# Attention rewritten inside an mLSTM and hash-routing kernel: masked exponents from one bf16 product, decay carried by q, cross term summed in PSUM, steps issued one ahead

## Chip, cores and metric

The kernel runs on one core of one Trainium2 chip. The metric is device time in microseconds (us), from launch to end. Three runs of the kernel before gave 596.22, 596.9 and 597.88 us, median 596.9.

## What is computed

Two blocks follow one another. The first is an mLSTM cell for 4 batches, 8 heads, 768 time steps and a head size of 40:

```python
m_new = maximum(f[t] + m, i[t])
f_stab, i_stab = exp(f[t] + m - m_new), exp(i[t] - m_new)
C = f_stab * C + i_stab * outer(v[t], k[t])
n = f_stab * n + i_stab * k[t]
y[t] = sigmoid(o[t]) * (C @ q[t]) / maximum(abs(n @ q[t]), 1)
```

The result, 3072 rows of 320 numbers, goes through the second block: `token_id * 2654435761 % 8` picks one of 8 experts for each row, and the row becomes `relu(x @ w1[e]) @ w2[e]` with w1 of 320x1024 and w2 of 1024x320. Everything is float32.

## The kernel before

**Attention (lines 104 to 486).** The recurrence is cut into chunks of 128 time steps, 6 chunks for each batch, so 24 steps (`for s in range(NT)`, line 476; b is the batch, c the chunk). A step treats all 8 heads of a chunk. Within a chunk the recurrence is a masked product: with A the running sum of the log decay and e the log input weight less A, the weight of source t' for target t is exp(A[t] + e[t']) where t >= t'. Between chunks a state C of 40x41 per head is carried (the 41st column is n, since v has a column of ones).

`gates()` (line 163) computes A, e and three exponentials with a head and batch on each of 32 partitions, 768 elements long, and turns them over with TensorE. A is kept as three bf16 pieces whose sum is the float32 value (`thirds`).

A step is issued as follows; one engine runs its own instructions in this order.

- `scores(s)`: eight products k q of 128x128 into PSUM (`sp`, line 264), the four even heads first and the four odd heads after them, 40 rows of the array each; VectorE multiplies them by the weights `w` (`p`, line 266).
- `transposes(s + 1)`: k and q of the next chunk, two heads at a time, eight transposes (`tr`, line 217), copied out by ScalarE (`kqT`, line 220).
- `decays(s + 1)`: eight bf16 products of 128 columns spread A over the partitions (`ab`, line 230); VectorE adds e (line 234), GpSimd cuts the triangle (line 238), ScalarE takes the exponential of 1024 elements (line 242). GpSimd weights k (`kw`, line 245). The output gate's sigmoid is built from a clip, an exponential, an addition and a reciprocal (`eo`, lines 251 to 254).
- `state(s)`: the cross term q C (`cx`, line 277) and the state's increment kw v (`cx`, line 284); VectorE scales the cross term (`hx`, line 287), GpSimd decays C (line 294), VectorE adds (line 303).
- routing work of the second block, hung on certain steps (`pieces`, line 466): constants at step 1, counts at 3, overflow at 4, slots at 5, four tables at 6 to 9 (`tk`, line 451), indices at 10, and the loads of three experts' weights at 12, 14 and 16.
- `attend(s)`: eight products p v (`hp`, line 311), 41 columns each; VectorE adds the cross term, makes the denominator (`den`) and multiplies twice; SyncE stores the 128 rows (`x_rows`).

A product of two float32 matrices takes two instructions; a transpose takes one. Loads are issued by SyncE (`load(s + 3)`, line 478), k, q, v and o in four transfers of 1024 rows of 160 bytes. The order is written out by hand (`manual_schedule`). SyncE waits for one thing at a time, so a load stands behind the store issued before it.

**Experts (lines 488 to 657).** Rows are gathered by index, turned over, sent through layer 1 (lines 529 and 536) and layer 2 (line 565), and scattered. At line 529 two products use 64 rows of the array each, upper and lower half by turns; at line 606 four products use 32 columns each by turns. w2 tiles come from a pool of 6 buffers.

Of the kernel before, what the change touches and what calls it, by code (L numbers as in the profile page):

```python
# [8 lines left out]
F32 = mybir.dt.float32  # L9
# [8 lines left out]
P = 128  # L18
# [4 lines left out]
def kernel(  # L23
# [36 lines left out]
    assert NB * P == S and FB * P == F and D <= DP and H % 2 == 0 and BH <= 32  # L60
# [17 lines left out]
    w2pool = ctx.enter_context(tc.tile_pool(name="w2pool", bufs=EG + 2))  # L78
# [8 lines left out]
    def weights(src1, src2):  # L87
# [13 lines left out]
    def load_weights(e):  # L101
        W[e] = weights(moe_w1[e], moe_w2[e])

    with tc.tile_pool(name="gates", bufs=1) as gp, \
# [4 lines left out]
        NKQ = 4  # L109
        kqs = [gp.tile([P, 2, H, DP], F32, name=f"kq{i}") for i in range(NKQ)]  # L110
        vs = [gp.tile([P, H, D1], F32, name=f"v{i}") for i in range(NKQ)]
        Cs = [gp.tile([P, PR, 2, D1], F32, name=f"C{i}") for i in range(2)]
        f_sb = gp.tile([BH, S], F32, name="f_sb")
        i_sb = gp.tile([BH, S], F32, name="i_sb")
        tok = gp.tile([P, NT], I64, name="tok")
        st = {}

        def load(s):
            b, c = s // NB, s % NB
            d = st[s] = {"kq": kqs[s % NKQ], "v": vs[s % NKQ]}  # L120
            d["o"] = ld.tile([P, H, D], F32, name="o_sb")
            for dst, src in (
                (d["kq"][:, 0, :, :D], k), (d["kq"][:, 1, :, :D], q), (d["v"][:, :, :D], v), (d["o"][:], o_gate),
            ):
# [3 lines left out]
        nc.scalar.dma_start(i_sb[:], i_gate.rearrange("b h s -> (b h) s"))  # L128
        nc.scalar.dma_start(tok[:], moe_token_ids.rearrange("(p t) -> p t", t=NT))
        make_identity(nc, ident[:])  # L130
        for t in kqs:
            nc.gpsimd.memset(t[:, :, :, D:], 0.0)
        for t in vs:
            nc.gpsimd.memset(t[:, :, D:], 1.0)
        for t in Cs:
            nc.gpsimd.memset(t[:], 0.0)
        for s in range(3):
            load(s)

        A_sb = gp.tile([BH, S], F32, name="A_sb")  # L140
        A3 = gp.tile([3 * 32, S], BF16, name="A3")
        sel3 = gp.tile([3 * 32, BH], BF16, name="sel3")
        e_T = gp.tile([P, NB, BH], F32, name="e_T")
        xA_T = gp.tile([P, NB, BH], F32, name="xA_T")
        kw_T = gp.tile([P, NB, BH], F32, name="kw_T")
        dec = gp.tile([P, BH // 2, NB], F32, name="dec")
# [4 lines left out]
        def thirds():  # L151

            nc.gpsimd.memset(sel3[:], 0.0)
            nc.gpsimd.memset(A3[:], 0.0)
            r1 = gp.tile([BH, S], F32, name="r1")
            r2 = gp.tile([BH, S], F32, name="r2")
            nc.vector.tensor_tensor(r1[:], A_sb[:], hi(A_sb), op=ALU.subtract)
            nc.vector.tensor_tensor(r2[:], r1[:], hi(r1), op=ALU.subtract)
            for i, piece in enumerate((hi(A_sb), hi(r1), r2[:])):
                nc.vector.tensor_copy(A3[32 * i : 32 * i + BH, :], piece)  # L160
                nc.vector.tensor_copy(sel3[32 * i : 32 * i + BH, :], ident[:BH, :BH])

        def gates():
            m_sb = gp.tile([BH, S], F32, name="m_sb")
            a_sb = gp.tile([BH, S], F32, name="a_sb")
            keep = gp.tile([BH, S], F32, name="keep")
            nc.vector.memset(keep[:], 1.0)
            nc.vector.memset(keep.rearrange("p (c t) -> p c t", t=P)[:, :, 0:1], 0.0)
            nc.vector.tensor_tensor_scan(m_sb[:], f_sb[:], i_sb[:], NEG, op0=ALU.add, op1=ALU.max)
            nc.vector.memset(a_sb[:, 0:1], 0.0)  # L170
            nc.vector.tensor_add(a_sb[:, 1:], f_sb[:, 1:], m_sb[:, : S - 1])
            nc.vector.tensor_sub(a_sb[:, 1:], a_sb[:, 1:], m_sb[:, 1:])
            nc.vector.tensor_tensor_scan(A_sb[:], keep[:], a_sb[:], 0.0, op0=ALU.mult, op1=ALU.add)
            thirds()
            e_sb, xA_sb, kw_sb = i_sb, f_sb, a_sb
            nc.vector.tensor_sub(e_sb[:], i_sb[:], m_sb[:])
            nc.vector.tensor_sub(e_sb[:], e_sb[:], A_sb[:])
            Ac = A_sb.rearrange("p (c t) -> p c t", t=P)
            nc.vector.tensor_tensor(
                kw_sb.rearrange("p (c t) -> p c t", t=P), e_sb.rearrange("p (c t) -> p c t", t=P),  # L180
                Ac[:, :, P - 1 : P].to_broadcast([BH, NB, P]), op=ALU.add,
            )
            nc.scalar.activation(kw_sb[:], kw_sb[:], AF.Exp)
            nc.scalar.activation(xA_sb[:], A_sb[:], AF.Exp)
            for src, dst in ((e_sb, e_T), (kw_sb, kw_T), (xA_sb, xA_T)):
                tp = ps.tile([P, NB, BH], F32, name="tpg", tag="tr", bufs=2)
                for c in range(NB):
                    nc.tensor.transpose(tp[:, c, :], src[:, c * P : (c + 1) * P], ident[:BH, :BH])
                nc.vector.tensor_copy(dst[:], tp[:])
# [286 lines left out]
        for s in range(NT):  # L476
            if s + 3 < NT:
                load(s + 3)
# [209 lines left out]
```

## Time and profile before

| what | value |
|---|---|
| median of three runs | 596.9 us |
| time of the profiled execution | 594.8 us |
| its span, first to last instruction | 593.1 us |
| PE busy | 515.4 us, 87% |
| DVE busy | 253.3 us, 43% |
| POOL busy | 131.0 us, 22% |
| ACT busy | 96.3 us, 16% |
| mean granted TensorE clock | 0.763 |

PE is TensorE's matmul side, PEld its weight loads, DVE VectorE, ACT ScalarE, POOL GpSimd, SP SyncE. Busy time counts a matmul from its start to its modelled end, so a busy PE may stand at half its clock. The granted clock is a share of 2.4 GHz; 0.50 is the level of 1.2 GHz.

### The profile page before, as it was taken

The page shows a single profiled execution, that of the slowest core. Times are in us where ns is not written, and L with a number is a line of the kernel's source. Part 1 is how long each engine was busy: PE and PEld are TensorE (multiplying, and loading weights), DVE is VectorE, ACT ScalarE, POOL GpSimd, SP SyncE. Part 2 cuts the span into 40 slices and gives each one's busy share as a digit, 9 for nine tenths or more (in the row PEclk, how much of TensorE's full clock was granted, in tenths as well). Part 3 has the DMA queues.
Part 4 walks back from the last instruction along what each step waited for, and adds up shares of the span by engine and source line. Part 5 has one row for each costly group of instructions (what it writes and reads, how often), then busy time and mean ns, then how long its engine had stood idle before and what let it go on. Part 6 is the DMA issues. An engine that isn't in the chain of part 4 may idle for free.

```text
span 593.1 us, 6980 instructions
## 1 busy us (share of the span) xinstructions
PE 515.4 (87%) x2678; PEld 402.6 (68%) x2678; DVE 253.3 (43%) x515; ACT 96.3 (16%) x167; POOL 131.0 (22%) x196
## 2 busy tenths in 40 slices
PE   0799598187669999999999489999999999999994
PEld 0699597177559999898999346565655666656553
DVE  7578568644463786878768321111111111111000
ACT  0331112010111122222221011101111011110110
POOL 2134211220221113221231240304131303010111
PEclk9995656555555656765565579999999999999998
DMA  9123223231122277894500124352513434000000
GB/s 175 17 53 61 55 56 56 55 56 29 28 56 55 56 194 156 228 262 82 102 22 11 55 78 135 110 167 88 188 56 104 145 108 137 11 21 12 22 12 23
DMA packets 120914, 49.52 MB, mean 83 GB/s; under 512 B 101804, under 2 KB 117168, under 8 KB 120880
## 3 DMA queue, kind: packets, MB, share of 16 engines
q1 hardware_dynamic: 118144, 40.64, 28.8%
q0 software_dynamic: 2496, 8.20, 4.4%
q8 instruction: 22, 0.36, 0.2%
q10 hardware_dynamic: 240, 0.22, 0.1%
q14 instruction: 12, 0.10, 0.0%
HBM read 41.18 MB, written 8.19 MB: 83 GB/s over the span
## 4 chain that ended last, share of the span: by engine, by line
PE 71%; DVE 14%; issue 5%; POOL 4%; ACT 3%; DMA 1%; POOLq 0%; ACTq 0%; DVEq 0%
PE mh L536 16%; PE zp L565 15%; PE hp L311 10%; PE sp L264 9%; PE tr L217 6%; PE mh L529 4%; DVE eo L254 4%; PE cx L277 3%; POOL w L238 2%; PE ab L230 2%; PE tk L451 2%; ACT w L242 2%; PE cx L284 1%; DVE w L234 1%; DVE p L266 1%
## 5 line engine op out<-in xcount | busy, mean ns | idle before, releaser
L565 PE MATMUL zp<-w2t,h 128*128 128x320 f32 x384 | 105.2, 433 | 0.0
L536 PE MATMUL mh<-xT,w1t 128*128 128x416 f32 x256 | 98.4, 528 | 0.9 <-issue 0.9
L565 PEld LDWEIGHTS zp<-w2t,h 128*128 128x128 f32 x384 | 72.7, 190 | 32.1 <-issue 3.3
L238 POOL TENSOR_SCALAR_AFFINE_SELECT w<-w 128x512 f32<-128x512 f32 x48 | 31.3, 675 | 227.9 <-DVE w L234 227.9
L311 PE MATMUL hp<-v,p 128*128 128x41 f32 x384 | 76.9, 380 | 2.0 <-DVE p L266 2.0
L536 PEld LDWEIGHTS mh<-xT,w1t 128*128 128x128 f32 x256 | 47.6, 193 | 44.0 <-issue 42.9
L311 PEld LDWEIGHTS hp<-v,p 128*128 128x128 f32 x384 | 73.8, 294 | 3.6 <-DVE p L266 2.5
L518 DVE COPY xT<-tp 128x384 f32<-128x384 f32 x16 | 8.9, 558 | 142.1 <-PE tp L514 102.7
L264 PE MATMUL sp<-kqT 40*128 40x128 f32 x384 | 69.1, 413 | 0.0
L264 PEld LDWEIGHTS sp<-kqT 40*128 40x128 f32 x384 | 62.2, 301 | 1.8 <-ACT kqT L220 0.2
L220 ACT COPY kqT<-tr 128x512 f32<-128x512 f32 x48 | 28.0, 585 | 167.8 <-PE tr L217 167.8
L254 DVE RECIPROCAL eo<-eo 128x320 f32<-128x320 f32 x24 | 51.7, 2153 | 0.8
L217 PE MATMUL tr<-ident,kq 128*128 128x128 f32 x192 | 46.3, 421 | 0.0
L499 POOL DMA_INDIRECT out_dram<-zo,s_idx x26 | 25.6, 985 | 92.6 <-ACT zo L498 92.6
L543 DVE TENSOR_SCALAR h<-mh 128x416 f32<-128x416 f32 x32 | 18.9, 592 | 53.4 <-PE mh L529 26.5
L217 PEld LDWEIGHTS tr<-ident,kq 128*128 128x128 f32 x192 | 36.9, 220 | 5.2 <-issue 5.1
L451 PE MATMUL tk<-oh_c,oh_r 128*128 128x47 f32 x48 | 11.2, 429 | 32.2 <-POOL oh_c L442 32.2
L242 ACT ACTIVATE w<-w 128x1024 f32<-128x1024 f32 x24 | 25.4, 1057 | 71.9 <-POOL w L238 71.9
L234 DVE TENSOR_TENSOR w<-ab,e_T 128x512 f32<-128x512 f32 x48 | 30.8, 684 | 13.9 <-PE ab L230 13.9
L277 PE MATMUL cx<-C,kqT 128*128 128x82 f32 x160 | 35.1, 392 | 0.1
L545 ACT ACTIVATE h<-mh 128x416 f32<-128x416 f32 x32 | 16.5, 517 | 109.6 <-PE mh L529 59.7
L277 PEld LDWEIGHTS cx<-C,kqT 128*128 128x128 f32 x160 | 33.1, 305 | 0.4 <-issue 0.4
(154 smaller groups left out, 442.8 us busy)
## 6 DMA issues: line engine op xcount, KB each, us to landing
w2t<-in_moe_w_dram SPq DMA_DIRECT2D x8, 1280.0 KB, 8.7
w1t<-in_moe_w_dram SPq DMA_DIRECT2D x8, 1024.0 KB, 5.3
kq<-in_k_dram SPq DMA_DIRECT2D x24, 160.0 KB, 2.8
kq<-in_q_dram SPq DMA_DIRECT2D x24, 160.0 KB, 3.4
v<-in_v_dram SPq DMA_DIRECT2D x24, 160.0 KB, 3.6
o_sb<-in_o_gate_dram SPq DMA_DIRECT2D x24, 160.0 KB, 3.6
x_rows<-x SPq DMA_DIRECT2D x24, 160.0 KB, 1.9
w1c<-in_moe_w_dram SPq DMA_DIRECT2D x16, 128.0 KB, 5.4
```

What stands on the lines that cost most here:

```text
L217: nc.tensor.transpose(tp[:, j, :], d["kq"][:, i, 2 * j : 2 * j + 2, :].rearrange("p h d -> p (h d)"), ident[:],)
L220: nc.scalar.copy(d["kqT"][:, i], tp[:])
L234: nc.vector.tensor_tensor(w[:, hf], ab[:], e_T[:, c, b * H + hf : (b + 1) * H : 2].unsqueeze(2).to_broadcast([P, PR, P]), op=ALU.add,)
L238: nc.gpsimd.affine_select(w[:, hf], w[:, hf], compare_op=ALU.is_ge, fill=NEG, base=0, pattern=[[0, PR], [1, P]], channel_multiplier=-1,)
L242: nc.scalar.activation(w[:], w[:], AF.Exp)
L254: nc.vector.reciprocal(d["eo"][:], d["eo"][:])
L264: nc.tensor.matmul(sp[:, j, :], lhsT=kqT[r, 0, j, :], rhs=kqT[r, 1, j, :], start=True, stop=True)
L277: nc.tensor.matmul(cx[:, 2 * j * D1 : (2 * j + 2) * D1], lhsT=d["kqT"][:, 1, j, :], rhs=st["C"][:, j].rearrange("p h d -> p (h d)"), start ...
L311: nc.tensor.matmul(hp[:, h, :], lhsT=d["p"][h % 2][:, h // 2, :], rhs=d["v"][:, h, :], start=True, stop=True)
L499: ins = nc.gpsimd.indirect_dma_start(out=out[:, :], out_offset=bass.IndirectOffsetOnAxis(ap=idx, axis=0), in_=zo[:], in_offset=None, bound ...
L536: nc.tensor.matmul(hp[i][:, :cols], lhsT=w1t[:, db, fb * P : (fb + 1) * P], rhs=xT[:, db, :cols], start=(first and db == 0), stop=(not fir ...
L565: nc.tensor.matmul(zp[:], lhsT=h[:, fb, j * P : (j + 1) * P], rhs=w[2][:, fb, :], start=(fb == 0), stop=(fb == FB - 1),)
```

## The change

- **Exponents and mask in one product.** `Ls` holds on its 128 partitions the pieces of e, rows of ones and a unit matrix; `Rs` holds a head selector, the pieces of A and a table of zeros and -1e30. Four bf16 products of 512 columns give A + e + mask for all heads (`ab`), each filling 64 of the 128 output partitions, and ScalarE takes the exponential straight from PSUM, twice 512 elements. The addition on VectorE and the cut on GpSimd go away. The pieces are written to DRAM (`z_d`) once by `gates()`; `load_e` reads e for each batch, `load_a` A for each step, two transfers.
- **Decay applied to q.** Two more products (`xb`) spread exp(A); VectorE multiplies the turned q by them (`qs`). ScalarE copies the last column as the decay of C (`dec`).
- **Cross term in PSUM.** In `attend(s)` each pair of heads gets the product qs C first and the two products w v are added in PSUM (`xh`, two buffers). `hx` goes away.
- **Scores by turns.** The eight products alternate between upper and lower 64 rows, and read 64 rows (24 of zeros) instead of 40.
- **Output gate.** ScalarE's Sigmoid on up to six chunks at once (five calls); GpSimd divides by the denominator (`gated`), VectorE makes the last product (`finish`).
- **q loaded by batch** in rows of 960 bytes. `pad_q` (VectorE, 320 elements) and `turn_q` take one sixth at a time: all six of batch 0 ahead of the loop, those of the next batch at chunks 0 to 4 of the batch before it (two at chunk 1).
- **Order.** In iteration s, `decays` and `scores` of s + 1 and the transposes of k of s + 2 stand ahead of `attend(s)`; `finish(s - 1)` and its store follow one iteration late. The routing pieces stand behind `attend(s)`.
- **Gates.** The maximum scan stays as it was; the rest runs on 96 partitions of 256 elements, after three transfers that spread m. `tables()` fills `Ls` and `Rs`.
- **w2 tiles** come from two pools of 3, the second opened after attention.

```diff
         def decays(s):
+            R = Rs[s % 2]
             for hf in range(2):
                 ab = ps.tile([P, PR, P], F32, name="ab", bufs=2)
-                for j in range(PR):
+                for i in range(2):
                     nc.tensor.matmul(
-                        ab[:, j, :], lhsT=sel3[:, bh : bh + 1].to_broadcast([3 * 32, P]),
-                        rhs=A3[:, c * P : (c + 1) * P], start=True, stop=True,
+                        ab[i * HB : (i + 1) * HB], lhsT=Ls[b % 2][:, c * P + i * HB : c * P + (i + 1) * HB],
+                        rhs=R[:, i, hf::2, :], start=True, stop=True,
                     )
-                nc.vector.tensor_tensor(
-                    w[:, hf], ab[:], e_T[:, c, b * H + hf : (b + 1) * H : 2].unsqueeze(2).to_broadcast([P, PR, P]),
-                    op=ALU.add,
-                )
-                nc.gpsimd.affine_select(
-                    w[:, hf], w[:, hf], compare_op=ALU.is_ge, fill=NEG,
-                    base=0, pattern=[[0, PR], [1, P]], channel_multiplier=-1,
-                )
-            nc.scalar.activation(w[:], w[:], AF.Exp)
+                nc.scalar.activation(w[:, hf], ab[:], AF.Exp)
+            if c > 0:
+                xb = ps.tile([P, PR, P], F32, name="xb", tag="tr", bufs=2)
+                for hf in range(2):
+                    nc.tensor.matmul(
+                        xb[hf * DP : (hf + 1) * DP], lhsT=Lx[:], rhs=R[:, 0, hf::2, :], start=True, stop=True,
+                    )
+                d["qs"] = wk.tile([P, PR, P], F32, name="qs")
+                nc.vector.tensor_tensor(d["qs"][:], q_of(s), xb[:], op=ALU.mult)
+                d["dec"] = wk.tile([P, PR, 1], F32, name="dec")
+                nc.scalar.copy(d["dec"][:], xb[:, :, P - 1 :])
-            nc.vector.tensor_scalar_max(d["eo"][:], d["o"][:], -88.0)
-            nc.scalar.activation(d["eo"][:], d["eo"][:], AF.Exp, scale=-1.0)
-            nc.vector.tensor_scalar_add(d["eo"][:], d["eo"][:], 1.0)
-            nc.vector.reciprocal(d["eo"][:], d["eo"][:])
...
         def scores(s):
+            for j in range(PR):
+                for hf in range(2):
+                    r = slice(hf * DP, (hf + 1) * DP)
+                    nc.tensor.matmul(
+                        sp[hf][:, j, :], lhsT=d["kT"][r, j, :], rhs=q_of(s)[r, j, :], start=True, stop=True,
+                    )
+            for hf in range(2):
+                nc.vector.tensor_tensor(d["w"][:, hf], sp[hf][:], d["w"][:, hf], op=ALU.mult)
...
         def attend(s):
+            for j in range(PR):
+                if c > 0:
+                    nc.tensor.matmul(
+                        d["xh"][:, 2 * j * D1 : (2 * j + 2) * D1], lhsT=d["qs"][:, j, :],
+                        rhs=st["C"][:, j].rearrange("p h d -> p (h d)"), start=True, stop=False, skip_group_check=True,
+                    )
+                for hf in range(2):
+                    nc.tensor.matmul(
+                        hs[:, 2 * j + hf, :], lhsT=d["w"][:, hf, j, :], rhs=d["v"][:, 2 * j + hf, :],
+                        start=(c == 0), stop=True, skip_group_check=True,
+                    )
+            nc.vector.tensor_scalar(den[:], hs[:, :, D:], scalar1=-1.0, scalar2=1.0, op0=ALU.mult, op1=ALU.max)
+            nc.vector.tensor_tensor(den[:], den[:], hs[:, :, D:], op=ALU.max)
+            nc.vector.reciprocal(den[:], den[:])
...
         for s in range(NT):
             if s + 3 < NT:
                 load(s + 3)
-            scores(s)
-            if s + 1 < NT:
-                transposes(s + 1)
-                decays(s + 1)
-            state(s)
-            for piece in pieces.get(s, []):
-                piece()
-            attend(s)
+            if s + 2 < NT:
+                load_a(s + 2)
...
+            decayed(s)
+            if s > 0:
+                gated(s - 1)
+            if s + 2 < NT:
+                turn_k(s + 2)
+            if b + 1 < B:
+                for r in turns_of.get(c, ()):
+                    pad_q(b + 1, r)
+                    turn_q(b + 1, r)
+            if s + 1 < NT:
+                decays(s + 1)
+            if s > 0 and (s, "all") in og:
+                sigmoid(s)
+            state(s)
+            if s + 1 < NT:
+                k_weights(s + 1)
+            if s > 0:
+                finish(s - 1)
+            if s + 1 < NT:
+                scores(s + 1)
+            attend(s)
+            for piece in pieces.get(s, []):
+                piece()
```

## Rows read from the trace of the kernel before

**Rows 1.** The page: the TensorE clock granted, in 40 slices of 14.8 us, tenths.

```profile
PEclk9995656555555656765565579999999999999998
```

**Rows 2.** The page: shares of the chain that ended last, by engine.

```profile
PE 71%; DVE 14%; issue 5%; POOL 4%; ACT 3%; DMA 1%; POOLq 0%; ACTq 0%; DVEq 0%
```

**Rows 3.** Stages: window and length, busy PE, PEld, DVE, ACT, POOL (instructions), PEclk, DMA, GB/s.

```profile
0.00:21.74 21.74, 3.03 (x20) 2.64 (x21) 14.49 (x25) 2.86 (x3) 3.63 (x18) 1.00 0.75 131
21.74:330.80 309.06, 268.30 (x1685) 254.36 (x1684) 205.60 (x410) 61.96 (x96) 71.10 (x110) 0.58 0.37 81
344.90:593.00 248.10, 240.36 (x962) 143.64 (x962) 29.00 (x67) 30.55 (x66) 49.07 (x60) 0.98 0.26 83
```

**Rows 4.** The chain through one step: start, us on the chain, work.

```profile
217.88 1.90 PE tr L217 x8
219.78 0.85 PE ab L230 x8
220.63 1.74 PE cx L277 x8
222.37 1.01 PE cx L284 x16
223.39 3.57 PE hp L311 x16
226.96 3.02 PE sp L264 x16
```

**Rows 5.** Order of time on PE, 229 to 240 us: start, us busy, work.

```profile
229.91 1.97 PE L217 MATMUL tr<-ident,kq 128*128 128x128 f32 x8
...
234.44 1.98 PE L311 MATMUL hp<-v,p 128*128 128x41 f32 x16
236.35 1.71 PE L264 MATMUL sp<-kqT 40*128 40x128 f32 x16
237.99 1.09 PE L217 MATMUL tr<-ident,kq 128*128 128x128 f32 x8
238.92 0.61 PE L230 MATMUL ab<-A,sel 96*128 96x128 bf16 x8
239.61 1.09 PE L277 MATMUL cx<-C,kqT 128*128 128x82 f32 x8
```

**Rows 6.** Two stretches around a rise of the clock, columns as in group 3.

```profile
229.80:233.20 3.40, 3.40 (x21) 3.23 (x20) 2.55 (x5) 1.17 (x2) 0.04 (x1) 0.50 0.52 109
233.20:236.60 3.40, 3.40 (x40) 3.22 (x40) 1.39 (x4) 1.42 (x2) 2.98 (x4) 1.00 0.75 134
```

**Rows 7.** The chain in the expert stage: products by turns on parts of the array.

```profile
453.72 4.44 PE zp L606 x64
458.16 8.81 PE zp L565 x32
478.13 1.60 PE mh L529 x8
```

**Rows 8.** Groups by line and shape: count | busy us, mean ns | idle before.

```profile
L254 DVE RECIPROCAL eo<-eo 128x320 f32<-128x320 f32 x24 | 51.7, 2153 | 0.8
L251 DVE TENSOR_SCALAR eo<-o_sb 128x320 f32<-128x320 f32 x24 | 10.3, 428 | 0.0
L321 DVE RECIPROCAL den<-den 128x8 f32<-128x8 f32 x24 | 4.9, 203 | 0.8
L242 ACT ACTIVATE w<-w 128x1024 f32<-128x1024 f32 x24 | 25.4, 1057 | 71.9 <-POOL w L238 71.9
L183 ACT ACT_TABLE_LOAD x1 | 1.3, 1283 | 2.5 <-issue 2.5
```

**Rows 9.** Order of time in step 6: a routing table's work on POOL and PE.

```profile
114.76 1.31 POOL L442 TENSOR_TENSOR oh_c<-oh_c,tokv 128x282 f32<-128x282 f32 x1 [4.05 <-DVE oh_c L438]
116.12 2.79 PE L451 MATMUL tk<-oh_c,oh_r 128*128 128x47 f32 x12 [14.51 <-POOL oh_c L442]
```

**Rows 10.** DMA issues: count, KB each, us from issue to landing.

```profile
w2t<-in_moe_w_dram SPq DMA_DIRECT2D x8, 1280.0 KB, 8.7
```

More of the change, by code (lines that the diff above doesn't have):

```diff
@@ L108 @@
          tc.manual_schedule():
-        NKQ = 4
-        kqs = [gp.tile([P, 2, H, DP], F32, name=f"kq{i}") for i in range(NKQ)]
-        vs = [gp.tile([P, H, D1], F32, name=f"v{i}") for i in range(NKQ)]
+        NC2 = NB // 2
+        BC = NC2 * BH
+        HB = P // 2
+        assert NC2 == 3 and BH == 32 and 3 * H <= 32 and DP == HB
+        NK = 4
+        ks = [gp.tile([P, H, DP], F32, name=f"k{i}") for i in range(NK)]
+        vs = [gp.tile([P, H, D1], F32, name=f"v{i}") for i in range(NK)]
@@ L133 @@
+        for t in ks[:3] + qps + kws + ks[3:]:
+            nc.gpsimd.memset(t[:, :, D:], 0.0)
         for t in vs:
@@ L136 @@
             nc.gpsimd.memset(t[:], 0.0)
+        for s in range(2):
+            load(s)
         for s in range(3):
[L138 to L146, printed above, removed]
+            load_o(s)
@@ L174, in gates, with pieces @@
[L174 to L178, printed above, removed]
+            tables()
+            def pieces(t, i0):
+                nc.vector.tensor_tensor(r1[:], t[:], hi(t), op=ALU.subtract)
+                nc.vector.tensor_tensor(r2[:], r1[:], hi(r1), op=ALU.subtract)
+                for i, piece in enumerate((hi(t), hi(r1), r2[:])):
+                    nc.scalar.copy(zt[:, i0 + i, :], piece)
+                nc.scalar.dma_start(z_d[:, i0 : i0 + 3, :], zt[:, i0 : i0 + 3, :])
@@ new lines, with pad_q, turn_q @@
+        nq = [0]
+        def pad_q(b, r):
+            t = qb[b][r] = qps[nq[0] % 2]
+            nq[0] += 1
+            nc.vector.tensor_copy(t[:, :, :D], qb[b]["l"][:, :, r * D : (r + 1) * D])
+        def turn_q(b, r):
+            if r == 0:
+                qb[b]["T"] = wk.tile([P, PR, S], F32, name="qT")
+            t = qb[b].pop(r)
+            tp = ps.tile([P, PR, P], F32, name="tr", tag="tr", bufs=2)
+            for j in range(PR):
+                nc.tensor.transpose(tp[:, j, :], t[:, 2 * j : 2 * j + 2, :].rearrange("p h d -> p (h d)"), ident[:])
+            nc.scalar.copy(qb[b]["T"][:, :, r::NB], tp[:])
@@ L471 @@
         }
+        turns_of = {0: (0,), 1: (1, 2), 2: (3,), 3: (4,), 4: (5,)}
         gates()
-        transposes(0)
+        load_a(0)
+        load_e(0)
+        load(2)
+        for r in range(NB):
+            pad_q(0, r)
+            turn_q(0, r)
+        nc.scalar.dma_start(tok[:], moe_token_ids.rearrange("(p t) -> p t", t=NT))
+        turn_k(0)
+        turn_k(1)
+        load_a(1)
+        load_q(1)
         decays(0)
+        k_weights(0)
+        sigmoid(0)
+        scores(0)
         for s in range(NT):
+            b, c = s // NB, s % NB
             if s + 3 < NT:
                 load(s + 3)
-            scores(s)
+            if s + 2 < NT:
+                load_a(s + 2)
+            for i in range(2):
+                o = s - (s - 3) % 6 + 6 + 2 * ((s - 3) % 6 - 1) + i if s > 2 else 3 + 2 * s + i
+                if o < NT and (s < 3 or 1 <= (s - 3) % 6 <= 3):
+                    load_o(o)
+            if c == 3 and b + 1 < B:
+                load_e(b + 1)
+            if c == 5 and b + 2 < B:
+                load_q(b + 2)
+            decayed(s)
[7 more added lines that the diff above has]
+                    turn_q(b + 1, r)
             if s + 1 < NT:
-                transposes(s + 1)
                 decays(s + 1)
+            if s > 0 and (s, "all") in og:
+                sigmoid(s)
             state(s)
+            if s + 1 < NT:
[5 more added lines that the diff above has]
+            attend(s)
             for piece in pieces.get(s, []):
                 piece()
-            attend(s)
+        gated(NT - 1)
+        finish(NT - 1)
+    w2pools.append(ctx.enter_context(tc.tile_pool(name="w2late", bufs=3)))
     xp = ctx.enter_context(tc.tile_pool(name="xp", bufs=2))
```

288 lines of the change are left out of this document (162 added, 126 removed).

## The prediction

> **What bounds the kernel now.** The chain that ended last is read first: 71% of the span is PE, 14% DVE [rows 2]. The stages come next [rows 3]. The experts' stage, from 344.90 to the end, has PE busy for 240.4 of 248.1 us at a granted clock of 0.98; the change doesn't touch it. The attention loop, 21.74 to 330.80, takes 309.1 us, with PE busy for 268.3 of them, but at a mean clock of 0.58. The slices of the page show it: 5 to 7 tenths through the loop, 9 after it [rows 1]. So the loop is bound by PE running mostly at the 1.2 GHz level, and the rest of its time is PE waiting.
>
> One step is then laid out. At the low level it is a closed row of PE work: 1.90 + 0.85 + 1.74 + 1.01 + 3.57 + 3.02 = 12.09 us [rows 4], the same kinds in every step. At the high level, start to start, hp takes 236.35 - 234.44 = 1.91, sp 1.64, tr 0.93, ab 0.69, and cx 1.09 by its busy time [rows 5]. So a step costs about half there, and what the change does to the clock is worth as much as what it does to the work.
>
> **The sum for the loop, part by part.** All of it is made against the profiled execution, 594.8 us, of which the span is 593.1; the median shown, 596.9, lies 2.1 us above, and these are added at the end.
>
> *Transposes.* Four of k and four of q, as before: 0.95 + 0.95 us low, 0.47 + 0.47 high. Six turns of q go ahead of the loop, so 18 are left in it.
>
> *Exponents (ab).* Before, eight bf16 products of 128 columns, 0.85 us low [rows 4], 0.83 ns a column. Now four of 512 columns, each on half of the array's columns. If two halves run beside one another, 2 x 512 x 0.83 = 0.85 us; one after another, 1.70. The trace shows such work side by side: the four products by turns on 32 columns each cost 4.44/64 = 69 ns apiece, the same 320 columns on the whole array 8.81/32 = 275 [rows 7], and the 16 products of cx at line 284, on 64 columns by turns, 63 ns apiece against hp's 223 [rows 4]. I take 0.85 low, 0.43 high. The two new products xb follow at 0.43 and 0.22.
>
> *Scores.* Four even heads and then four odd ones took 3.02. By turns on the upper and lower 64 rows the nearest row is line 529, 416 columns by halves in 1.60/8 = 200 ns, less than the 275 of 320 columns on the whole array [rows 7]. So 3.02/2 = 1.51 low, 0.82 high; the upper end is no gain at all, 3.02 and 1.64.
>
> *Cross term, increment, hp.* The same products in another order: 1.74, 1.01 and 3.57 low; 1.09, 0.50 (half of 1.01) and 1.91 high.
>
> A full step is thus 11.0 us low and 5.9 high. For the loop, with xb and cross term in 20 steps and the increment in 20: high 24 x (0.47 + 0.43 + 0.82 + 1.91) + 18 x 0.47 + 20 x (0.22 + 1.09 + 0.50) = 87 + 8 + 36 = **131**; low 165 + 17 + 64 = **246**.
>
> *What the other engines must hide.* DVE is busy for 205.6/24 = 8.6 us a step [rows 3]; the reciprocal (2.15) and the clip (0.43) alone [rows 8] bring it to 6.0, and the additions at line 234 go too, so about 5 is left and fits beside 5.9, barely. The cut on POOL leaves the path between product and exponential; POOL keeps three short products. ACT has two copies and two exponentials of 512 elements (under 0.6 each by the 1.057 of 1024) and a share of the sigmoids, 3.5 in all. These edits I cost at nothing while a step lasts 5.9.
>
> The sigmoid makes ACT load its tables anew: five calls, there and back, 10 x 1.28 = 13 us by the row [rows 8], which lie beside PE, as no PE work of the same step waits for a sigmoid. The Trainium skill, in "ScalarE: Activation LUTs", section "What ACT_TABLE_LOAD costs", speaks against this part: exp and sigmoid are in different sets, and a switch costs 2.66 us with its drain. By the page that is 27 us instead of 13; were none of it hidden, the sum would be 542 by the page and 528 by the row. The row shows the 1.28 and no drain.
>
> *A new wait on PE.* `turn_q` waits for `pad_q` on DVE, and that stands behind `den(s - 1)`, which waits for the end of `attend(s - 1)`. Three small operations (0.20 each), the copy of 320 elements (0.43) [rows 8] and some 0.4 of product tail and handoffs, 1.4 us, of which `turn_k` covers 0.47: 1.0 us at 15 steps = **15**. Queued behind `pad_q` are qs, the state's addition and the score product, none needed by PE before the next step.
>
> *Routing pieces, now behind attend.* Tables: PE waits for den (0.6), the compare (0.43), POOL's 1.31 and handoffs, 2.5, then tk takes 2.79 [rows 9]: 5.3 x 4 = 21. At step 6 the wait was 14.51 before. Counts (four operations, a product, a copy) 2.7, slots (ten operations of 192 elements at 0.43 or less) 4.3; constants, overflow and indices fall where PE has no turn of q behind them. Together **28**.
>
> *Start.* Iteration 0 needs w(0). The maximum is spread by transfers, two on SyncE behind some 2.1 MB of loads, which at the stage's 131 GB/s [rows 3] is up to 16 us; I take m at 14. ACT fills the tables (about 8 us by 1.057 per 1024), then makes nine copies of pieces, the exponentials and eight copies of turns; the pieces go to DRAM and come back. I take the loop's start at **33**, between 26 (tables covered by the wait) and 40; now it is 24.5, 21.74 and the first transposes and products.
>
> *Loads.* One step of lead is gone. v(s + 3) waits for attend(s - 1), and k(s + 4), A and o stand behind the store of `finish(s - 1)`. At 12, 14 and 16 they stand behind expert weights (8.7 us to land [rows 10]), against 1.5 steps of lead, about 9 us. I take **5**, between 0 and 30.
>
> *The clock.* Ahead of the rise at 233.20 [rows 6] PE ran transposes [rows 5], then ab and cx without a gap. The new step has these, xb, and scores on both halves of the rows at once, in one stretch, so I expect rises in the first steps and after each stop. In the steps with the longest waits (3 to 10) I expect it to fall again. I take seven steps' worth at the low level, 7 x (11.0 - 5.9) = **36**, between 0 and 115 (all).
>
> Sum: the loop ends at 33 + 131 + 15 + 28 + 5 + 36 = **248** instead of 330.8. What follows (den, gated, last product, store, gathers) is as long as before within 0.5. That is 83 us less: 594.8 - 83 = 512, and with 2.1 and rounding **515**.
>
> **The rivals.** *The clock stays low.* For it: 0.58 now, with PE hardly pausing; the new wait comes once a step. Then 33 + 246 + 15 x 0.5 + 28 + 5 = 320, 586 us (570 to 602). Against it: the rises at 233.20 and elsewhere came from the work that is kept. The Trainium skill, "TensorE: Matmul & The Clock Gate", Part 4 on PE-mode transpose, has a rule that leads here: the full rate does not engage for transposes, as they are not counted as busy in the same way. By that rule the turns bring no rise; the trace disagrees, since the rise came behind eight of them. Chance 0.11.
>
> *Halves one after another* (slower). In ab, xb and sp: at the low level 24 x (0.85 + 1.51) + 20 x 0.43 = 65 more than all-low, 385 and **651** us; at the high level 34 more, 549. It makes the kernel slower once PE is low in about 6 steps of 10; now it is in 8 of 10. Rows 7 and the 63 ns speak against it [rows 4, 7]. Chance 0.05.
>
> *Loads come late.* If each weight load costs 10 us and k, A and o are late elsewhere, 30 instead of 5: 540. For it: SyncE's queue is blocked once a step by the store. Against: DMA share is 0.37 in the loop [rows 3]. Chance 0.10.
>
> *It doesn't do what it says*: routing pieces and `pad_q` still hang on DVE's queue, so PE waits on in the 15 steps. That is in the sum, and in the first rival's size.
>
> **How the numbers follow.** My forecast has 0.74, mostly 490 to 550. The range, 488 to 562, adds late loads and serial halves at the high clock, and half of the loop at the low one (61 instead of 36 us: 540); it leaves out the low-clock case and the slower one. A measurement of this kernel tells apart about 0.3%. Low clock gives half of its 0.11 to faster at least (0.07), 0.02 to same, 0.02 to slower; so faster 0.91, same 0.02, slower 0.07.
>
> **What would show it.** In the changed profile: the loop's end near 248, PEclk mostly 1.00 in it after the first steps; ab as four products with two starting together; sp near half of its time; attend unchanged; PE idle about 1 us before `turn_q`, released by `pad_q`; idle of 2 to 3 us before tk; ACT with 11 table loads and no PE wait on them. Wrong, if PEclk stays near 0.5, if sp still takes 3.0 at the low level, if PE waits for DMA in most steps, or if the first `attend` comes later than 42.

## The result and the profile after

Four runs of the changed kernel gave 497.6 to 505.6 us, median **500.5 us**, beside 596.6 us for the kernel before (four runs): ratio 0.837 (0.833 to 0.842), 96 us less. The forecast, 515 us with a range of 488 to 562, held.

The page of the kernel after, the granted clock in 40 slices of 12.4 us and the chain's shares by engine:

```profile
PEclk9999976677787898799589999999999999999997
...
PE 69%; issue 10%; DMA 8%; DVE 6%; POOL 3%; ACT 2%; SPq 1%; POOLq 0%; ACTq 0%; DVEq 0%
```

Where 5 to 7 tenths stood all through the loop [rows 1], 6 to 9 stand now, and DVE's share of the chain is 6% instead of 14% [rows 2]. DMA and issue have grown.

The stages of the kernel after, columns as in group 3 of the rows above:

```profile
0.00:31.43 31.43, 8.54 (x34) 6.15 (x34) 15.44 (x36) 20.41 (x29) 6.43 (x24) 1.00 0.65 153
31.43:231.00 199.57, 164.54 (x1561) 141.34 (x1561) 99.67 (x261) 77.91 (x124) 48.05 (x82) 0.84 0.52 121
...
249.30:497.00 247.70, 240.21 (x962) 143.63 (x962) 28.98 (x67) 30.56 (x66) 49.05 (x60) 0.98 0.26 83
```

The last row answers to the last of [rows 3]: the experts' stage is as before, 247.7 against 248.1 us, but starts at 249.3 instead of 344.9. So all that changed lies ahead of it. The preparation takes longer: the first score product starts at 32.0 instead of 24.5 us. From there to the last product of `attend` it is 203.2 us instead of 306.3. The same window view over exactly this stretch, called the loop from here on, splits it; before first, then after:

```profile
24.50:330.80 306.30, 265.54 (x1669) 251.86 (x1668) 205.02 (x409) 60.79 (x94) 71.10 (x110) 0.58 0.37 82
32.00:235.20 203.20, 168.17 (x1594) 145.27 (x1592) 100.89 (x265) 77.45 (x124) 48.77 (x83) 0.84 0.51 120
```

PE is busy for 168.2 us instead of 265.5 and idle for 35.0 instead of 40.8. **PE waits hardly less; it does its work in 97 us less**, at a granted clock of 0.84 instead of 0.58.

One step of the kernel after at the high level, PE's instructions in order of time (start, us, work):

```profile
216.11 0.63 PE L285 MATMUL tr<-ident,k 128*128 128x128 f32 x4
216.67 0.62 PE L316 MATMUL ab<-R,L 128*64 128x512 bf16 x4
217.13 0.38 PE L324 MATMUL xb<-R,Lx 128*64 128x512 bf16 x2
217.34 0.61 PE L382 MATMUL xh<-v,kw 128*64 128x41 f32 x16
217.89 1.16 PE L353 MATMUL sp<-qT,kT 64*128 64x128 f32 x16
218.98 0.45 PE L396 MATMUL xh<-C,qs 128*128 128x82 f32 x2
219.26 0.58 PE L401 MATMUL xh<-v,w 128*128 128x41 f32 x4
...
221.68 0.63 PE L285 MATMUL tr<-ident,k 128*128 128x128 f32 x4
```

From start to start: turns of k 0.56, exponents 0.46, `xb` 0.21, increment 0.55, scores 1.09, `attend` 2.70, a step without a turn of q of 221.68 - 216.11 = 5.57 us. The four products of `ab` take 0.46 us at the high level, near the 0.43 that the forecast has for two halves side by side, so the halves run beside one another.

PE's waits from 31 to 240 us of the kernel after (who waits for whom: us in total, times, longest):

```profile
PE tr L301 <- DVE qp L293: 13.8, 8, 6.2
PE tk L544 <- POOL oh_c L535: 9.6, 4, 2.4
PE tr L285 <- DMA k<-in_k_dram: 7.5, 3, 3.1
PE cps L477 <- DVE pr L472: 2.4, 1, 2.4
PE tr L301 <- ACT kT L286: 1.5, 2, 0.8
```

These sum to 34.8 us, nearly all of the loop's idle time. Before, the tables' wait was up to 14.5 us a time [rows 9] and 32.2 us in all by the same view; now it is 2.4 a time, and new waits for `pad_q` and for k have come.

### The profile page after: what moved, and what is told of

It is laid out like the page before. It is cut to its first block, busy times and chain, and to the rows that moved or that the text cites. A ratio compares the mean times of both kernels' runs of the same rounds, so it can differ in the third digit from the quotient of the medians.

```text
span 497.6 us, 6769 instructions
## 1 busy us (share of the span) xinstructions
PE 421.3 (85%) x2604; PEld 297.2 (60%) x2604; DVE 148.7 (30%) x379; ACT 129.8 (26%) x221; POOL 112.1 (23%) x176
## 4 chain that ended last, share of the span: by engine, by line
PE 69%; issue 10%; DMA 8%; DVE 6%; POOL 3%; ACT 2%; SPq 1%; POOLq 0%; ACTq 0%; DVEq 0%
PE mh L673 19%; PE zp L702 18%; PE mh L666 5%; PE xh L401 5%; PE sp L353 4%; PE xh L396 3%; PE ab L316 3%; PE tr L301 3%; DMA R<-gate_pieces 2%; PE xh L382 2%; PE tk L544 2%; PE tr L285 2%; DMA k<-in_k_dram 2%; DMA ql<-in_q_dram 1%; PE tp L649 1%
## 5 line engine op out<-in xcount | busy, mean ns | idle before, releaser
L401 PE MATMUL xh<-v,w 128*128 128x41 f32 x384 | 54.1, 275 | 0.0
L401 PEld LDWEIGHTS xh<-v,w 128*128 128x128 f32 x384 | 49.8, 193 | 0.7 <-issue 0.4
L301 PE MATMUL tr<-ident,qp 128*128 128x128 f32 x96 | 20.9, 368 | 17.0 <-DVE qp L293 15.0
L396 PE MATMUL xh<-C,qs 128*128 128x82 f32 x160 | 34.7, 299 | 0.0
L357 DVE TENSOR_TENSOR w<-sp,w 128x512 f32<-128x512 f32 x48 | 30.8, 683 | 11.1 <-PE sp L353 9.7
L353 PE MATMUL sp<-qT,kT 64*128 64x128 f32 x384 | 32.3, 315 | 0.0
L302 ACT COPY qT<-tr 128x512 f32<-128x512 f32 x24 | 25.2, 1092 | 17.6 <-PE tr L301 17.6
L413 POOL TENSOR_TENSOR og<-og,den 128x320 f32<-128x320 f32 x24 | 17.4, 724 | 54.6 <-DVE den L410 43.8
L353 PEld LDWEIGHTS sp<-qT,kT 64*128 64x128 f32 x384 | 27.5, 217 | 2.9 <-issue 0.4
L328 DVE TENSOR_TENSOR qs<-qT,xb 128x512 f32<-128x512 f32 x20 | 13.8, 688 | 44.5 <-PE xb L324 44.5
L666 PE MATMUL mh<-xT,w1c 64*128 64x416 f32 x128 | 26.7, 535 | 0.0
```

The costliest lines, as they stand in the source:

```text
L301: nc.tensor.transpose(tp[:, j, :], t[:, 2 * j : 2 * j + 2, :].rearrange("p h d -> p (h d)"), ident[:])
L302: nc.scalar.copy(qb[b]["T"][:, :, r::NB], tp[:])
L353: nc.tensor.matmul(sp[hf][:, j, :], lhsT=d["kT"][r, j, :], rhs=q_of(s)[r, j, :], start=True, stop=True,)
L357: nc.vector.tensor_tensor(d["w"][:, hf], sp[hf][:], d["w"][:, hf], op=ALU.mult)
L396: nc.tensor.matmul(d["xh"][:, 2 * j * D1 : (2 * j + 2) * D1], lhsT=d["qs"][:, j, :], rhs=st["C"][:, j].rearrange("p h d -> p (h d)"), star ...
L401: nc.tensor.matmul(hs[:, 2 * j + hf, :], lhsT=d["w"][:, hf, j, :], rhs=d["v"][:, 2 * j + hf, :], start=(c == 0), stop=True, skip_group_che ...
```

## The experiments

The theory of the forecast: the gain is PE's time, shorter scores and above all a higher clock, and VectorE's work costs nothing beside it. The rivals: the gain is the order and VectorE's relief, with PE's own change a small part of it; or the clock answers to something else, such as the rows that the scores read. Ratios are to the kernel before, run on the same chip. The table has, for every kernel, what the window view gives from the first score product to the last of `attend`, in one profiled run of it.

| kernel | time, us | ratio (95%) | loop, us | PE busy | PE idle | clock | DVE busy |
|---|---|---|---|---|---|---|---|
| before | 596.6 | 1 | 306.3 | 265.5 | 40.8 | 0.58 | 205.0 |
| e3_before_64_rows | 591.1 | 0.992 (0.989 to 0.994) | 303.2 | 246.2 | 57.0 | 0.64 | 204.5 |
| e4_before_turns | 585.3 | 0.984 (0.978 to 0.991) | 296.6 | 222.7 | 74.0 | 0.66 | 204.0 |
| e12_before_turns_sigmoid | 523.0 | 0.875 (0.868 to 0.882) | 233.3 | 205.7 | 27.7 | 0.68 | 141.1 |
| after | 500.5 | 0.837 (0.833 to 0.842) | 203.2 | 168.2 | 35.0 | 0.84 | 100.9 |
| e1_heads_in_order | 520.8 | 0.867 (0.857 to 0.877) | 235.9 | 204.3 | 31.6 | 0.75 | 101.6 |
| e2_scores_40_rows | 511.0 | 0.862 (0.854 to 0.869) | 208.1 | 171.7 | 36.4 | 0.83 | 100.5 |
| e5_gate_on_vector | 605.6 | 1.014 (1.007 to 1.020) | 309.2 | 235.6 | 73.6 | 0.64 | 162.8 |
| e8_finish_at_once | 542.6 | 0.912 (0.905 to 0.919) | 241.4 | 179.8 | 61.6 | 0.77 | 100.5 |
| e9_scores_in_own_step | 562.5 | none | 266.4 | 216.0 | 50.4 | 0.67 | 100.9 |
| e11_increment_apart | 529.5 | 0.885 (0.879 to 0.891) | 236.1 | 196.0 | 40.1 | 0.74 | 100.6 |
| e6_pad_early | 488.2 | 0.819 (0.814 to 0.824) | 193.0 | 163.3 | 29.7 | 0.87 | 99.2 |
| e7_tables_early | 485.7 | 0.816 (0.811 to 0.821) | 189.5 | 158.1 | 31.4 | 0.89 | 101.8 |
| e10_all_three | 471.9 | 0.791 (0.786 to 0.795) | 175.3 | 156.6 | 18.7 | 0.90 | 99.0 |

The four runs of e9 lie too far apart (550.8 to 572.3 us) for an interval, and its row of the loop is that of a run of 561 us. Those of e1 span 18 us, and its row is that of a run of 531 us, the longest. The row of e2 is that of its shortest run, 505 us.

**Scores by turns, undone in the changed kernel.**

```diff
-            for j in range(PR):
-                for hf in range(2):
+            for hf in range(2):
+                for j in range(PR):
                     r = slice(hf * DP, (hf + 1) * DP)
                     nc.tensor.matmul(
                         sp[hf][:, j, :], lhsT=d["kT"][r, j, :], rhs=q_of(s)[r, j, :], start=True, stop=True,
```

> The changed kernel with the scores back to four even heads and then four odd ones (still 64 rows each). Theory A (the clock): most of the gain is TensorE's clock, which rises since the step's products now stand in one stretch; the scores by turns are worth their own PE time only. Then sp goes from about 1.1 back to 1.65-1.9 us at the high level, 24 x 0.8 = 20 us more, the clock in the loop stays near 0.84: 515 to 530 us. Rival C (the turns): the two halves side by side are what keeps the array full and the clock high; without them the clock in the loop drops towards 0.6 and the time to 550 us or more.

20 us slower. The groups by line of both kernels (line, tile, count | us busy, mean ns) show the direct part; first after, then e1:

```profile
L353 PE MATMUL sp<-qT,kT 64*128 64x128 f32 x384 | 32.3, 315 | 0.0
```

```profile
L353 PE MATMUL sp<-qT,kT 64*128 64x128 f32 x384 | 49.4, 323 | 0.0
```

One product lasts as long, but side by side they fill 32.3 us instead of 49.4. That is 17 of the 36 us by which PE is busier in this run; the rest goes with the clock, 0.75 instead of 0.84. Over the whole span this run lists 0.866, the other three 0.882 to 0.908 and the runs of the kernel after 0.907 to 0.919, so the median run lost less. The time came out as the theory expected (515 to 530 us), but the clock did not stay where it was.

**Rows that the scores read**, 40 instead of 64 in the kernel after, and 64 instead of 40 in the kernel before:

```diff
-                    r = slice(hf * DP, (hf + 1) * DP)
+                    r = slice(hf * DP, hf * DP + D)
```

> The changed kernel with the scores by turns reading 40 rows each instead of 64 (the 24 rows left out hold zeros, so the result is the same). The matmuls take as long per instruction. Theory A1 (rows do not matter to the clock): 500 us within 1%, clock in the loop 0.84 within 0.03. Rival A2 (the clock follows how many rows of the array work): clock in the loop 0.75 or lower, 510 to 530 us.

> The kernel before with its scores reading 64 rows (24 of zeros) instead of 40, in the old order. PE's work takes exactly as long at either level. A1 (rows do not matter): 596.5 us within 0.5%. A2 (the clock follows the rows): granted clock in the loop above 0.63 instead of 0.58, 560 to 588 us. Under the rival that the changed kernel's gain is pauses taken out, nothing changes here either.

Both move the same way, and neither meets one of its expectations in full. 40 rows cost the changed kernel some 10 us (the intervals 0.854 to 0.869 and 0.833 to 0.842 don't meet). The loop's clock is 0.83 instead of 0.84 in its shortest run; over the whole span the other three runs list 0.876 to 0.881, the four of the kernel after 0.907 to 0.919. 64 rows of which 24 are zeros give the kernel before 5 us, with the clock in its loop at 0.64 instead of 0.58 and products about as long (405 ns against 413 by the groups). Over the whole span all ten runs of e3 list 0.793 to 0.816, and twelve of the thirteen runs of the kernel before beside them 0.752 to 0.791; the thirteenth lists 0.919 at 600.0 us, so the listed clock of one run alone shows little. In e3 PE is busy for 19 us less but idle for 16 more. So quicker PE work is mostly eaten by something else there.

**Turns alone, in the kernel before**, and then the sigmoid on ScalarE beside it:

```diff
             for hf in range(2):
-                r = slice(hf * DP, hf * DP + D)
-                for j in range(PR):
-                    nc.tensor.matmul(sp[:, j, :], lhsT=kqT[r, 0, j, :], rhs=kqT[r, 1, j, :], start=True, stop=True)
...
+            for j in range(PR):
+                for hf in range(2):
+                    r = slice(hf * DP, hf * DP + D)
+                    nc.tensor.matmul(sps[hf][:, j, :], lhsT=kqT[r, 0, j, :], rhs=kqT[r, 1, j, :], start=True, stop=True)
```

```diff
-            nc.vector.tensor_scalar_max(d["eo"][:], d["o"][:], -88.0)
-            nc.scalar.activation(d["eo"][:], d["eo"][:], AF.Exp, scale=-1.0)
-            nc.vector.tensor_scalar_add(d["eo"][:], d["eo"][:], 1.0)
-            nc.vector.reciprocal(d["eo"][:], d["eo"][:])
+            nc.scalar.activation(d["eo"][:], d["o"][:], AF.Sigmoid)
```

> The kernel before with nothing but the scores by turns (40 rows). Work: sp from 3.02 to 1.5 us at the low level, in 24 steps 36 us; some of it is lost where PE then waits for VectorE (steps 3 to 9). Theory A: 560 to 575 us and the clock in the loop near 0.6. Rival C (turns make the gain): 530 us or less and the clock above 0.75. Rival B (the gain is pauses taken out, PE's work does not matter): over 585.

> The kernel before with two small parts of the change: scores by turns (e4) and the output gate by ScalarE's sigmoid instead of four operations, three of them VectorE's. VectorE loses 2.9 us a step of 8.6; ScalarE changes its table twice a step. Theory B (VectorE's queue was the second bound): e4's 585 falls to 525 to 555 us. Theory A (PE and its clock alone): 570 to 585. If the table loads come onto the path: over 585.

PE's waits in the loop of e4:

```profile
PE tk L452 <- POOL oh_c L443: 35.1, 4, 14.3
PE hp L312 <- DVE p L267: 17.3, 22, 4.0
PE cx L278 <- DVE C L304: 11.9, 6, 2.8
```

and of e12:

```profile
PE tk L449 <- POOL oh_c L440: 18.8, 4, 9.1
...
PE hp L309 <- DVE p L264: 3.2, 9, 1.1
```

This is the pair that decides. Turns alone take 43 us from PE's busy time, and 33 come back as idle time, most of it waits for VectorE (17.3 us for `p` and 11.9 for C, where the kernel before has 2.0 and none): it stood just behind PE all along, hidden by PE's longer work. Without the clip, the addition and the reciprocal the waits for `p` fall to 3.2 us, those for C vanish, the tables' fall from 35.1 to 18.8, and 62 us more go. The two small parts together give 74 of the 96 us, and that with a clock of 0.68 in the loop, not 0.84. The other 22 us came with the rest of the change. No run takes its product for the exponents, the decay on q or the cross term in PSUM by itself, so what each of these gives is not shown.

**The old gate in the changed kernel.** e5 makes the output gate of each step on VectorE again, in the changed order.

```diff
-            o = og[s, "all"]
-            nc.scalar.activation(o, o, AF.Sigmoid)
+            o = og[s]
+            nc.vector.tensor_scalar_max(o, o, -88.0)
+            nc.scalar.activation(o, o, AF.Exp, scale=-1.0)
+            nc.vector.tensor_scalar_add(o, o, 1.0)
+            nc.vector.reciprocal(o, o)
```

> The changed kernel with the output gate built step by step as before: clip, addition and reciprocal on VectorE, one exponential on ScalarE, no sigmoid. VectorE gets 0.43 + 0.37 + 2.15 = 2.9 us a step more, 70 us in all, on top of about 100 us in a loop of 204. Theory A (PE sets the step, VectorE has room): 500 to 512 us. Theory B (VectorE's queue in order is a second bound close behind PE, as the 11 us out of 36 in the kernel before with scores by turns suggest): PE waits for VectorE in most steps, 530 to 575 us.

The whole gain goes, and the kernel is 1% slower than the one before, beyond the 530 to 575 us expected if VectorE's queue was the second bound. One step of e5 in order of time:

```profile
189.38 1.16 PE L356 MATMUL sp<-qT,kT 64*128 64x128 f32 x16
...
190.56 2.15 DVE L348 RECIPROCAL og<-og 128x320 f32<-128x320 f32 x1
192.63 0.60 DVE L391 TENSOR_TENSOR C<-C,xh 64x164 f32<-64x164 f32 x2
...
193.28 0.72 PE L399 MATMUL xh<-C,qs 128*128 128x82 f32 x2 [2.74 <-DVE C L391]
```

The increment is done as the scores start, but its addition to C stands behind the reciprocal in VectorE's queue, and PE, ready at about 190.5, waits 2.74 us for it. In the loop the waits for this addition come to:

```profile
PE xh L399 <- DVE C L391: 39.8, 16, 3.5
```

The loop is 106 us longer than in the kernel after: PE is idle for 39 us more, and its own work takes 67 us more, at a clock of 0.64 instead of 0.84. VectorE is busy for only 162.8 of 309 us: not its load, but what stands ahead in its order, makes PE wait.

**Finishing a step in its own iteration** (`gated` and `finish` right behind `attend`):

```diff
-            if s > 0:
-                gated(s - 1)
...
-            if s > 0:
-                finish(s - 1)
...
             attend(s)
+            gated(s)
+            finish(s)
```

> The changed kernel with gated(s) and finish(s) straight behind attend(s) instead of one iteration late. VectorE then waits for GpSimd's 0.72 us and handoffs (1.0 to 1.4 us) ahead of pad_q and of the routing pieces. Theory B: PE waits that much longer at the 15 steps with a turn of q and in the routing steps, 15 to 30 us more and a lower clock: 515 to 535 us. Theory A (PE's own work sets the step): 498 to 506 us.

42 us slower. Waits in the loop of e8, PE's and VectorE's own:

```profile
PE tr L301 <- DVE qp L293: 24.9, 8, 7.3
DVE x L418 <- POOL og L413: 19.5, 23, 0.9
PE tr L285 <- DMA k<-in_k_dram: 15.8, 5, 8.4
PE tk L544 <- POOL oh_c L535: 15.1, 4, 3.8
```

VectorE's last product now stands in its queue waiting for GpSimd, 0.85 us in each of 23 steps; `pad_q` and the tables behind it come later, and PE with them (24.9 instead of 13.8, 15.1 instead of 9.6). The loads of k are late for 15.8 us instead of 7.5. PE idles for 27 us more and is busy for 12 more, at 0.77.

**Scores in their own step** instead of one ahead (e9: `scores(s)` first in iteration s), and then the increment in a PSUM tile of its own (e11):

```diff
+            scores(s)
             decayed(s)
...
-            if s + 1 < NT:
-                scores(s + 1)
             attend(s)
```

```diff
-                dC = xh[:, LH : LH + LC].rearrange("p (j d) -> p j d", d=D1)
+                dC = ps.tile([P, PR, D1], F32, name="dC", tag="sp0")
```

> The changed kernel with scores(s) at the head of iteration s instead of ahead of attend(s - 1): this undoes the step ahead for the scores alone. The score product on VectorE (1.3 us) now stands ahead of pad_q and has only the transposes, ab, xb and the increment to hide behind. My sum: 0.7 us more wait at 15 steps, 8 to 18 us more, 508 to 518 us. If the step ahead is what takes PE's pauses out, 530 us or more. If it does nothing: 500 us within 1%.

> e9 (scores in their own step) with the state's increment kw v in a PSUM tile of its own (scores' first buffer) instead of the end of xh. In e9 PE waits at 16 steps about 0.9 us at the head of attend for VectorE's addition of the increment, though attend reads an older state. If that wait, through the shared tile, is how e9 loses its 62 us (the clock falling with it): 500 to 520 us. If the loss comes from the score product standing ahead of pad_q: 545 us or more.

One step of e9 in order of time:

```profile
201.63 0.89 PE L382 MATMUL xh<-v,kw 128*64 128x41 f32 x16
...
202.64 0.66 DVE L388 TENSOR_TENSOR C<-C,xh 64x164 f32<-64x164 f32 x2
...
203.36 0.45 PE L396 MATMUL xh<-C,qs 128*128 128x82 f32 x2 [0.84 <-DVE C L388]
```

and this wait in the whole loop of e9:

```profile
PE xh L396 <- DVE C L388: 14.0, 16, 0.9
```

`attend(s)` reads the state of the step before, so by its arithmetic it needs nothing of this addition. But its products write into the PSUM tile `xh` from which VectorE is still reading the increment, and they wait until it has read. In the kernel after, the scores of the next step stand between the two:

```profile
100.31 0.52 PE L382 MATMUL xh<-v,kw 128*64 128x41 f32 x12
...
100.76 1.16 PE L353 MATMUL sp<-qT,kT 64*128 64x128 f32 x16
...
101.03 0.65 DVE L388 TENSOR_TENSOR C<-C,xh 64x164 f32<-64x164 f32 x2
...
101.85 0.45 PE L396 MATMUL xh<-C,qs 128*128 128x82 f32 x2
```

The addition ends at 101.68, the scores at about 101.85: covered with 0.2 us to spare. With the increment in a tile of its own this wait is gone from e11's list, and 33 of the 62 us come back by the medians, or 21 of 50 if e9 is taken at its shortest run. The rest is not explained by it: e11 falls between the two outcomes expected of it. In e9's profiled run the idle time grows by only 15 us, but the clock falls to 0.67 and PE is busy for 48 us more, so the time is far above the 508 to 518 us of the sum made for it; and in e11 a wait of 14.0 us in all gives back 33 (or 21) when it goes. Whether the pauses alone hold the clock down, or also the new order of PE's work, these runs don't tell apart.

**The three waits that are left, taken one by one and together.** e6 issues `pad_q` an iteration earlier, behind `finish`, and loads q at chunk 2 instead of 5. e7 makes the one-hot rows of a table ahead of `scores(s + 1)` and only their product behind `attend`. e10 has both (the rows right behind `scores`) and loads the experts' weights at steps 19 to 21 instead of 12, 14 and 16.

```diff
+            b1, c1 = (s + 1) // NB, (s + 1) % NB
+            if b1 + 1 < B:
+                for r in turns_of.get(c1, ()):
+                    pad_q(b1 + 1, r)
             if s + 1 < NT:
                 scores(s + 1)
+            if 6 <= s <= 9:
+                oh = route_table(s - 6)
             attend(s)
...
-            9: [lambda: route_table(3)], 10: [route_index],
-            12: [lambda: load_weights(0)], 14: [lambda: load_weights(1)], 16: [lambda: load_weights(2)],
+            9: [lambda: route_sum(3, oh)], 10: [route_index],
+            19: [lambda: load_weights(0)], 20: [lambda: load_weights(1)], 21: [lambda: load_weights(2)],
```

> The changed kernel with pad_q issued one iteration earlier, ahead of the score product and of den, and the load of q for the next batch but one at chunk 2 instead of chunk 5. If the wait of turn_q for pad_q is what PE loses between steps (0.5 to 1.0 us at 15 steps, 6.2 behind the slots of step 5, 4.6 at step 12 for q's load): 13 to 25 us less, 477 to 489 us. If PE then waits for the next thing on VectorE (qs, the state's addition): less than 6 us gained.

> The changed kernel with each routing table's comparisons (VectorE) and product (GpSimd) issued ahead of attend and only the twelve matmuls behind it. PE then no longer waits 2.4 us for GpSimd at steps 6 to 9 (9.6 us in the trace). Small sum: 10 us of waits and some of the clock that falls in these four steps: 478 to 490 us. If the clock does not rise in these steps: 488 to 492. If the comparisons on VectorE only move the wait to the score product: 497 to 503.

> pad_q and q's load early (e6), the tables early, and the expert weights loaded at steps 19, 20 and 21 instead of 12, 14 and 16 (k and the pieces of A waited for some 17 us of DMA behind them). If the three are independent: 12 from e6, 10 to 20 from the tables, 8 to 15 from the loads: 455 to 472 us. If the late weights delay the first expert, over 475.

Each shortens the loop by more than PE's idle time falls. e7 saves 13.7 us of loop with only 3.6 us less idle time: the tables' 9.6 us of waits are gone, but those for k and for ScalarE's copy of it grow from 9.0 to 15.0, and the clock goes from 0.84 to 0.89. PE's waits in the loop of e10:

```profile
PE tr L285 <- DMA k<-in_k_dram: 4.6, 1, 4.6
PE xh L401 <- DVE C L386: 4.5, 1, 4.5
...
PE tk L548 <- POOL oh_c L535: 2.1, 3, 0.7
```

The wait for `pad_q` (13.8) is down to 1.2, the tables' from 9.6 to 2.1, that for k from 7.5 to 4.6. The second line is new: with `pad_q` out of the way, the next thing that PE needs from behind the routing's slots in VectorE's queue is the first state of a batch, copied out of PSUM, and PE waits 4.5 us for that. **e10 beats both kernels**: 471.9 us, some 28 less than the change.

## Why the prediction was right, and where it was wrong

**The size and the main step were right.** The forecast took 83 us off the loop's end; it came at 235.2 instead of 330.8, 96 less, and nothing after it moved. The time came where it was expected, from PE's work done at the high level. Term by term:

| term | forecast, us | measured, us |
|---|---|---|
| loop start | 33 | 32.0 |
| a step at the high level without a turn of q (5.9 - 0.47) | 5.4 | 5.57 |
| of it: scores, `attend` | 0.82, 3.00 | 1.09, 2.70 |
| wait for `pad_q` | 15 | 13.8 + 1.5 |
| wait ahead of a table's product | 2.5 | 2.4 |
| k and q late | 5 | 7.5 + 4.6 |
| low clock | 36 | at most 33 |
| loop's end | 248 | 235.2 |

The last-but-one is worked out: a mean clock of 0.84 means that 2 x (1 - 0.84) = 0.32 of 203.2 us, 65 us, stood at the low level, and work done there takes twice as long, so half of it at most was lost. The clock is lowest where I had put it, around the routing pieces (0.71 from 62 to 112 us by the window view), but from there to 231 us it is 0.85, so it came back less fully than I had said. To find the 13 us by which the loop ended earlier, the sum is split into PE's work and PE's waits. It has 131 + 36 + 4 x 2.79 = 178 us of work, and PE was busy for 168.2; it has 15 + 5 + 28 - 11 = 37 us of waits, and PE was idle for 35.0. So 10 of the 13 us are work, 2 waits and 1 the start. Within a step two errors cancel, which is luck: the turns save a third of the scores' time (1.64 to 1.09 us), not half, and `attend` takes 0.30 us less than the sum of its parts.

**`pad_q`: right in sum, wrong in make-up.** I had 1.0 us at each of 15 steps. There were 8 waits, and the ordinary one is half of that; two of them carry the sum (PE, order of time):

```profile
84.34 1.09 PE L301 MATMUL tr<-ident,qp 128*128 128x128 f32 x4 [6.20 <-DVE qp L293]
...
153.78 1.08 PE L301 MATMUL tr<-ident,qp 128*128 128x128 f32 x4 [4.57 <-DVE qp L293]
...
179.37 0.63 PE L301 MATMUL tr<-ident,qp 128*128 128x128 f32 x4 [0.51 <-DVE qp L293]
```

At 84.34 VectorE had the slots of the routing ahead of it; at 153.78 `pad_q` itself waited for the load of q. The 4.57 is therefore a late load, which I had sized at 5 in all: with k it is 12.

**The step that failed** is the sentence on what stands behind `pad_q`: "Queued behind `pad_q` are qs, the state's addition and the score product, none needed by PE before the next step", and with it "These edits I cost at nothing". The state's addition is awaited in the same step, by the first product of `attend`, through the shared PSUM tile; what covers it is the scores put ahead, 1.1 us long. So the parts that I took for free, or gave no price of their own, hold the gain up. With the old gate e5 loses 105 us against the change, without the scores ahead e9 loses 50 to 72, with `finish` in its own iteration e8 loses 42. I had said VectorE "fits beside 5.9, barely", by its busy time; in e5 it is busy for 162.8 / 24 = 6.8 us a step, yet a step takes 12.9. At half its time busy it can still set the pace. I weighed each edit against PE's work alone, and that gave the right sum only since the change takes all of them at once.

**The clock.** I expected it to fall with the waits and come back after them, and so it does. What I did not say is how it multiplies a small wait: in e9's profiled run 15 us more of idle time went with 48 us more of PE time.

**The rivals.** *The clock stays low* fell: 0.84, and 500 us instead of 586. The rule by which the Trainium skill ("TensorE: Matmul & The Clock Gate", Part 4 on PE-mode transpose) led there, that the full rate does not engage for transposes, does not hold here. The start of the kernel after on PE:

```profile
22.65 1.94 PE L301 MATMUL tr<-ident,qp 128*128 128x128 f32 x8 [1.16 <-DVE qp L293]
...
29.46 2.04 PE L285 MATMUL tr<-ident,k 128*128 128x128 f32 x8 [0.23 <-ACT qT L302]
31.43 0.62 PE L316 MATMUL ab<-R,L 128*64 128x512 bf16 x4
```

Eight turns in 2.04 us are the low level, as in [rows 5] at 229.91 (the clock column has 1.00 there, but the durations are those of the low level), and `ab` at 31.43 lasts as long as at 216.67 in the high-level step. PE had done nothing but transposes since 22.65 when the clock rose. The row that I set against the rule in the prediction is weaker than I said: between the eight transposes at 229.91 and the rise at 233.20 PE ran `ab` (from 231.67) and began `cx` (at 232.52). *Halves one after another* fell: `ab` 0.46 us for four products, and undoing the turns costs e1 17 us of score time. *Loads come late* was partly so, 12 us instead of 5 and not 30. *It doesn't do what it says*: PE does still hang on DVE's queue, but for 13.8 us, and 9.6 + 2.4 in the routing pieces.

**ScalarE's tables** cost nothing, as taken. The eleven loads stand in the groups by line of the kernel after:

```profile
L345 ACT ACT_TABLE_LOAD x5 | 6.4, 1283 | 0.1
L320 ACT ACT_TABLE_LOAD x5 | 6.4, 1283 | 0.1
L219 ACT ACT_TABLE_LOAD x1 | 1.3, 1283 | 6.3 <-DVE one L215 6.3
```

No PE wait is for them. Of the drain that the Trainium skill counts beside each load ("ScalarE: Activation LUTs", "What ACT_TABLE_LOAD costs") the trace shows nothing: a load of 1.28 us that starts at 58.24 is followed by its sigmoid at 59.54. e12 switches 47 times, 60 us of ScalarE by 1283 ns each, and is still 62 us faster than e4: where ScalarE has room, even this is cheaper than the three operations on VectorE.

## What to carry to other kernels

Ahead of costing an edit at nothing, ask not whether the engine has time left but what stands ahead in its queue of the one instruction that the bound engine waits for next, and count reads of a shared PSUM tile as such a wait. Where PE moves between its two clock levels, a wait of under 1 us in each step can cost more than its length (14.0 us of it in e9 cost 33 by the medians, 21 at the least), so work put between producer and consumer can pay more than the idle time shows. When one engine's work is cut and the time hardly moves, look for the engine that stood just behind it (e4), and cut both (e12).

## What the runs showed of the hardware that was not expected

**A strided copy on ScalarE took nearly twice as long.** Two copies of the same size from PSUM, in the groups by line of the kernel after; the first writes every sixth element, 24 bytes apart, the second a row without gaps:

```profile
L302 ACT COPY qT<-tr 128x512 f32<-128x512 f32 x24 | 25.2, 1092 | 17.6 <-PE tr L301 17.6
L286 ACT COPY kT<-tr 128x512 f32<-128x512 f32 x24 | 14.0, 584 | 101.9 <-PE tr L285 101.9
```

I had both under 0.6. The Trainium skill has a rule that fits ("SBUF — State Buffer", the note on cachelines): accesses that leave a 16-byte line each time pay a penalty. No run here writes q without the stride, so the cause is not shown.

**Rows of zeros went with a higher clock.** In e3 the 24 added rows hold zeros and the products last about as long, yet the clock in the loop goes from 0.58 to 0.64, and in e2, with the rows taken away, the time is 10 us longer and three of four runs list a lower clock than any run of the kernel after. That the rows read count is what the two share; how, stays open.
